# Overlapping slices, powers on GpSimd and half swaps by DMA in a fused scan-and-gate kernel

## The chip, the cores and the metric

The kernel runs on one core of one Trainium2 chip. The core has five engines that matter here. TensorE (PE in the profile) multiplies 128-row tiles and leaves sums in PSUM. VectorE (DVE) and ScalarE (ACT) do elementwise work. GpSimd (POOL) does small elementwise work. SyncE (SP) issues transfers. Each has its own stream of instructions, and they meet only through semaphores. The metric is the time of one execution on the device in microseconds; of the kernel before there are three runs, and one more execution was recorded by the profiler.

## What is computed

```python
xn = layernorm(x)                                  # x: 2048 x 448, bf16
# the scan (448 complex states, diagonal)
dt      = exp(log_dt);  Lam_bar = exp(dt * Lam)
B_bar   = ((Lam_bar - 1) / Lam)[:, None] * B
h[t]    = Lam_bar * h[t-1] + B_bar @ xn[t]
s       = 2 * real(C @ h) + xn * Dskip
# the gate (two dense layers of 448 -> 1792 -> 448)
g       = silu(gelu(layernorm(xn) @ w1 + b1) @ w2 + b2)
out     = x + s * g
```

The second layernorm of an already normed row differs from the first only in its factor, since `eps` enters twice. So the kernel takes the mean and variance of x once and forms two factors from them. The rows scaled by the first factor (`xn`) go into the scan, those scaled by the second (`xm` in the names, `xn2` in the buffers) into the gate.

## The kernel before

**Tiles.** The 2048 rows are worked on in four groups `g` of 512. A group is two blocks `b` of two tiles `r` with 128 rows each. The width 448 is three and a half tiles of 128. Where it is the contracted dimension, columns 0 to 383 fill three tiles, and the last 64 columns stand in the fourth tile twice, once in each half of the partitions. `halved` (L663) then runs the product in pairs of matmuls on 64 of the 128 partitions: a first pass over all four tiles for one half, a second over three for the other, so that the 64 doubled columns count once. It serves the w1 products (`mm1`, `mm1_half`) and the first three tiles of the B projection (`bu`).

**The doubled columns** come from more transfers and copies: `ldxe` loads columns 384 to 447 of x a second time, `dup` (L432) copies them on GpSimd for the first tiles, `ldw1` (L381) loads the last 64 rows of w1 in two transfers for each of four chunks, and the tails of B are loaded narrow, doubled on GpSimd, and transposed by a DMA of their own in `bt` (L638).

**Stages of a group.** The norms (`ln_stats`, `ln_scale`, `ln_apply`; `first_norm` for the first block of group 0); transposes of xn and xm (`xt`), by TensorE or by a transposing DMA; the B projection in four steps (`bu`, named `U{g}{i}`); the scan (`ssm`): two products of all states with cosine and sine tables `WT`, a sum, seven scans along the 512 rows (L710), a copy of the scanned states to bf16 (`s_b`, L715), two products back and a sum into `h_sb`; the w1 products in seven steps of two column tiles each (`mm1`, named `H{g}{j}`; for group 0 in halves, `H0{j}{b}`), each followed by gelu on ScalarE into `gT`; the w2 products (`mm2`, 14 matmuls of 448 columns for each tile of rows, L777) after a pair of small matmuls that put b2 in the bank (L772), then silu; and the outputs (`ym`): seven matmuls with `CQ` and four with the diagonal tiles `DG` of Dskip (L798, L801), times g, plus x, and a store.

**The fourth tile of states** holds only 64 complex states. Their real part fills one half of the partitions and their imaginary part the other. A complex product then needs the two halves in swapped places as well. Before, ScalarE makes the swapped copy by two half copies of 64 partitions: from PSUM after `bu(g, 3)` (L692, L693), and from `s_f` after the scan (L717, L718). `bu(g, 3)` is eight half-column matmuls (L689).

**Parameters.** `parameters` (L522) turns the vectors by tiny matmuls and works out the decay and the angle of each state, mostly on GpSimd: exp(dt) and the modulus `R1` by Exp on ScalarE (L539, L546), sines by a polynomial. `first_norm` forms 1/sqrt(variance) by Ln and Exp on ScalarE (L446, L447), `ln_scale` by a power on GpSimd (L477) or by an iteration on VectorE. `tables` (L596) makes `WT` on VectorE and by five Sin instructions on ScalarE. Ln/Exp, gelu and sine/silu belong to three table sets of ScalarE, and each change of set is an `ACT_TABLE_LOAD`.

**Order.** Each call only records a `Task` with what it reads and writes. `emit` then issues the tasks in the order of a list written out by hand, `ORDER`. An entry is the number of a task, or its name: `H{g}{j}`, `U{g}{i}`, `T0` (transposes of `first_norm`), `I0` and `I1` (matmuls on zeros, with no reader), `ST` and `DH`. Each engine works through its own tasks in that order. `SECOND` lists the tasks that take their second alternative, for instance VectorE in place of ScalarE. `BANKS` gives each PSUM tile its bank. A task waits for the last of what it depends on, the earlier users of its bank among it. SP issues nearly all transfers, in the order of the list. So one that waits holds those behind it.

Of the kernel before, what the change touches and what calls it, by code (L numbers as in the profile page):

```python
# [200 lines left out]
18 ST I0 0 10 12 1 24 19 14 17 23 22 29 30 31 20 28 21 27 83 84 25 44 13 26 16 15 82 89 90 32 33 34 42 88 2 3 4 85 91 86 T0 94 92 T1 35 41  # L201
43 36 47 45 87 7 I1 40 38 39 93 H040 98 97 100 H050 114 H010 46 63 96 48 116 99 101 102 103 H000 115 37 108 117 H020 106 H030 79 95 109 110
104 107 111 H060 112 136 134 135 118 113 171 137 8 53 119 105 5 49 50 52 H051 H001 130 131 11 242 H011 120 H021 122 139 H031 124 121 51 H041
123 126 125 241 6 H061 155 170 127 138 158 159 62 143 141 142 140 144 128 129 161 55 56 57 58 218 160 162 132 246 243 240 247 245 133 146
145 148 223 221 224 244 147 54 329 248 333 327 149 153 150 258 225 259 151 157 156 226 219 220 227 U02 U00 193 152 U01 249 252 189 191 328
331 255 250 251 326 253 254 222 330 61 64 DH 68 173 194 154 192 H11 332 256 H16 71 334 190 292 415 414 257 413 172 165 338 H13 163 174 167
H14 293 296 419 412 297 417 197 198 260 298 418 302 H15 168 195 303 299 166 335 300 164 H12 196 65 H10 294 78 416 199 60 339 U12 206 290 265
301 295 U10 304 291 203 266 336 66 67 69 72 73 70 75 74 77 76 204 205 U11 207 202 261 340 80 175 344 177 262 169 200 337 178 201 176 208 209
214 181 309 263 307 310 311 211 179 264 308 305 213 420 180 183 312 H26 H22 388 210 182 185 306 H20 215 184 270 313 H25 376 216 186 217 421
269 422 389 345 380 H23 271 377 187 188 386 381 382 424 59 212 425 267 9 81 234 230 268 383 277 236 387 278 228 341 276 274 279 342 275 423  # L210
426 H32 346 237 272 231 H33 464 466 235 H31 229 H35 273 462 281 285 280 465 467 463 343 282 U22 286 U20 351 287 347 352 238 U21 470 349 288
232 348 H21 239 289 350 283 471 356 H30 H24 378 379 460 284 H34 384 461 385 395 468 355 357 360 353 316 322 314 354 320 396 363 361 362 398
364 365 323 358 317 430 427 428 429 359 321 431 432 315 366 U32 U31 437 469 367 371 397 399 372 368 U30 324 373 374 438 369 370 435 433 436
434 442 375 H36 474 390 472 473 479 325 233 393 439 441 440 443 318 447 450 406 475 476 394 400 408 451 448 446 449 444 453 407 445 452 454
319 455 456 402 480 391 477 392 457 458 459 482 403 401 404 405 484 483 481 478 409 486 485 410 490 411 487 488 491 492 494 495 489 493 496
498 499 500 501 497
""".split()]
SECOND = [int(k) if k.isdigit() else k for k in """
45 135 212 248 258 259 284 334 335 336 338 339 341 342 344 345 370 421 422 427 428 430 431
""".split()]  # L220
BANKS = [int(k) if k.isdigit() else k for k in """
0 3 1 0 2 0 6 2 6 4 0 4 0 2 6 0 2 4 6 4 0 6 4 0 4 2 3 4 5 2 6 3 7 0 6 4 2 6 2 0 4 6 2 0 2 3 4 5 7 5 4 6 4 6 0 4 2 0 6 0 6 4 0 6 7 0 1 2 7 3
4 0 6 4 2 4 6 0 4 2 2 2 4 5 0 1 2 3 2 0 1
""".split()]
B2_PE = tuple(range(16))


LN_EPS = 1e-5
# [8 lines left out]
def bass_recurrent_scan__ssm_conv_s5__mixer_channel_mlp__prompt_kernel(  # L237
# [14 lines left out]
    NB, NG, NF, NK = 8, 4, 14, 512  # L252
# [3 lines left out]
    with ExitStack() as es:  # L256
# [3 lines left out]
        ident = SB("ident", [128, 128])  # L260
        still = SB("still", [128, 128])
        mhalf = SB("mhalf", [128, 1, 1], F32)
        sgn = SB("sgn", [128, 4], F32)
        cw = SB("cw", [128, 26, 4], F32)

        ang = SB("ang", [128, 5, 2, 2, 4], F32)
# [64 lines left out]
        with nc.Block():  # L331
# [42 lines left out]
            def ldxe(b0, n, reads=()):  # L374
                ldx(b0, n, reads, True)
# [528 lines left out]
```

## Time and profile before

| | us |
|---|---|
| three runs: median (lowest to highest) | 151.18 (150.34 to 151.41) |
| the profiled execution: its span | 148.9 |
| median less span | 2.3 |
| 0 to 7.96 us: PE / ACT / DVE / POOL busy | 5.29 / 4.22 / 4.74 / 3.06 |
| 7.96 to 21.00 us | 12.99 / 10.27 / 10.13 / 5.10 |
| 21.00 to 42.80 us | 20.97 / 21.68 / 12.91 / 6.46 |
| 42.80 to 138.60 us | 95.77 / 82.12 / 94.32 / 30.48 |
| 138.60 to 148.90 us | 7.57 / 1.42 / 6.80 / 0.00 |

The profiled execution has no device time of its own beside its span; the span begins and ends with the first and last recorded work, and the device time of a run also holds what lies around it. The stretches are cut where the first w1 matmul starts (7.96), at the end of the first w1 stage (21.00), where VectorE starts the products of the scan (42.80) and where the last state is nearly done (138.60). The costliest groups of instructions in the page, beside those shown with the prediction, are these:

```profile
L668 PE MATMUL psum<-xn2T,w_sb 64*128 64x512 bf16 (+1 forms) x490 | 46.3, 342 | 1.1 <-DVE lnmv L429 1.1
...
L710 DVE TENSOR_TENSOR_SCAN s_f<-cw,cur,v_sb 128x512 f32<-128x512 f32 x21 | 25.3, 1265 | 0.5 <-POOL cur L728 0.4
L798 PE MATMUL psum<-CQ,h_sb 128*128 128x448 bf16 (+2 forms) x119 | 24.7, 342 | 0.0
L668 PE MATMUL psum<-xnT,BT 64*128 64x512 bf16 x168 | 19.8, 377 | 0.5 <-DMA BT<-in_A_B_im_dram 0.4
```

Left of the bar stand the line, the engine, the operation, the written tile and the read tiles, the sizes and the count. Then come the busy time of the group in us, the mean of one in ns, and the idle time of the engine ahead of the group with what ended most of it. The w1 products (46.3 us), the w2 products (43.4 us), the outputs (24.7 us) and the B projection (19.8 us) are TensorE's work; the scans on VectorE are 25.3 us of its 128.9.

### The profile page before, as it was taken

How to read it: one execution, taken by the hardware profiler on the slowest of the kernel's cores; microseconds unless marked ns; L12 is line 12 of the kernel's file. 1: busy time of each engine (PE TensorE's matmuls, PEld its weight loads, DVE VectorE, ACT ScalarE, POOL GpSimd, SP SyncE). 2: the span in 40 equal slices, each digit the busy share in tenths (PEclk: the TensorE clock that was granted, in tenths of full speed). 3: DMA queues.
4: the chain of work that ended last, by engine and by line, in shares of the span. 5: the costliest groups of instructions: out<-in, count | busy, mean ns of one | idle time of the engine just before them, and what ended most of it. 6: DMA issues, size and time to landing. Idle time of an engine off the chain costs nothing.

```text
span 148.9 us, 3017 instructions
## 1 busy us (share of the span) xinstructions
PE 142.6 (96%) x1156; PEld 77.3 (52%) x1156; DVE 128.9 (87%) x198; ACT 119.7 (80%) x181; POOL 45.1 (30%) x84
## 2 busy tenths in 40 slices
PE   7789989998999999999999999999999999999992
PEld 2378975544554445545455545545544445555562
DVE  2983999950479999999999999989999999999874
ACT  2738999999999999999999999989799855291300
POOL 3360547800004999996000000930003700000000
PEclk9959999999999999999999999999999999999999
DMA  4789999969988530000324301000702101000033
GB/s 108 206 251 233 343 255 142 149 117 178 189 144 124 105 72 0 0 0 4 70 45 95 70 4 61 0 7 0 141 0 67 62 0 62 0 0 4 8 118 123
DMA packets 32767, 13.25 MB, mean 89 GB/s; under 512 B 25960, under 2 KB 32368, under 8 KB 32752
## 3 DMA queue, kind: packets, MB, share of 16 engines
q1 hardware_dynamic: 32592, 12.98, 41.9%
q8 instruction: 9, 0.15, 0.4%
q10 hardware_dynamic: 160, 0.07, 0.2%
q14 instruction: 6, 0.05, 0.1%
HBM read 5.82 MB, written 1.84 MB: 51 GB/s over the span
## 4 chain that ended last, share of the span: by engine, by line
PE 78%; ACT 7%; POOL 4%; DVE 4%; DMA 2%; issue 2%; ACTq 1%; SPq 1%; DVEq 0%; POOLq 0%
PE psum L668 37%; PE psum L777 21%; PE psum L798 14%; ACT gT L761 5%; PE psum L689 3%; DMA BT<-in_A_B_im_dram 2%; PE psum L801 2%; ACTq L107 1%; POOL cw L564 1%; SPq L106 1%; ACT L341 1%; DVE t L804 1%; DVE lnst L425 1%; PE psum L772 1%; DVE tmp L808 1%
## 5 line engine op out<-in xcount | busy, mean ns | idle before, releaser
L668 PE MATMUL psum<-xn2T,w_sb 64*128 64x512 bf16 (+1 forms) x490 | 46.3, 342 | 1.1 <-DVE lnmv L429 1.1
L777 PE MATMUL psum<-w_sb,gT 128*128 128x448 bf16 x224 | 43.4, 353 | 0.4 <-DMA w_sb<-in_B_w_dram 0.4
L668 PEld LDWEIGHTS psum<-xn2T,w_sb 64*128 64x128 bf16 x490 | 28.0, 110 | 17.5 <-issue 1.3
L777 PEld LDWEIGHTS psum<-w_sb,gT 128*128 128x128 bf16 x224 | 21.6, 98 | 21.5 <-DMA w_sb<-in_B_w_dram 0.8
L749 ACT ACTIVATE gT<-psum,b1f 128x512 bf16<-128x512 f32 x42 | 25.5, 689 | 0.4 <-PE psum L668 0.3
L710 DVE TENSOR_TENSOR_SCAN s_f<-cw,cur,v_sb 128x512 f32<-128x512 f32 x21 | 25.3, 1265 | 0.5 <-POOL cur L728 0.4
L798 PE MATMUL psum<-CQ,h_sb 128*128 128x448 bf16 (+2 forms) x119 | 24.7, 342 | 0.0
L668 PE MATMUL psum<-xnT,BT 64*128 64x512 bf16 x168 | 19.8, 377 | 0.5 <-DMA BT<-in_A_B_im_dram 0.4
L725 POOL TENSOR_TENSOR cwk<-s_f,ang 128x8 f32<-128x8 f32 x3 | 4.2, 1408 | 39.7 <-ACT s_f L722 39.5
L715 ACT ACTIVATE s_b<-s_f 128x3072 bf16<-128x3072 f32 x4 | 11.0, 2760 | 4.7 <-DVE s_f L710 4.7
L798 PEld LDWEIGHTS psum<-CQ,h_sb 128*128 128x128 bf16 x119 | 10.4, 98 | 7.4 <-issue 0.5
L425 DVE BATCH_NORM_STATS2 lnst<-x_all 128x6 f32<-128x448 bf16 x14 | 8.1, 612 | 6.8 <-DMA x_all<-in_A_x_dram 6.8
L668 PEld LDWEIGHTS psum<-xnT,BT 64*128 64x128 bf16 x168 | 8.1, 94 | 10.8 <-issue 1.6
L781 ACT ACTIVATE g_sb<-psum 128x448 bf16<-128x448 f32 x16 | 8.0, 537 | 6.7 <-PE psum L777 6.7
L761 ACT ACTIVATE gT<-psum,b1f 128x256 bf16<-128x256 f32 x28 | 11.1, 471 | 2.8 <-PE psum L668 2.8
L685 ACT ACTIVATE u_sb<-psum 128x1024 bf16<-128x1024 f32 x12 | 11.8, 1025 | 0.2
L564 POOL TENSOR_TENSOR cw<-cw 128x4 f32<-128x4 f32 x11 | 4.8, 445 | 19.7 <-DVE lnmv L429 17.0
L804 DVE TENSOR_TENSOR t<-psum,g_sb 128x448 bf16<-128x448 f32 (+2 forms) x17 | 9.7, 589 | 1.3 <-PE psum L798 1.3
L499 ACT ACTIVATE xn_sb<-x_all,lnw 128x512 bf16<-128x512 bf16 x13 | 10.3, 809 | 0.1
L710 DVE TENSOR_TENSOR_SCAN s_f<-cw,v_sb 128x512 f32<-128x512 f32 x7 | 8.2, 1213 | 0.0
L498 DVE TENSOR_SCALAR xn_sb<-x_all,lnw 128x512 bf16<-128x512 bf16 x17 | 6.5, 404 | 1.5 <-issue 1.3
L732 DVE TENSOR_TENSOR pa<-s_b,WT 128x3072 bf16<-128x3072 bf16 x4 | 7.0, 1750 | 0.4 <-ACT s_b L715 0.4
(131 smaller groups left out, 184.7 us busy)
## 6 DMA issues: line engine op xcount, KB each, us to landing
out_dram<-tmp SPq DMA_DIRECT2D x7, 224.0 KB, 2.1
x_all<-in_A_x_dram SPq DMA_DIRECT2D x3, 448.0 KB, 5.3
w_sb<-in_B_w_dram SPq DMA_DIRECT2D x3, 448.0 KB, 8.2
w_sb<-in_B_w_dram SPq DMA_DIRECT2D x3, 384.0 KB, 4.8
w_sb<-in_B_w_dram SPq DMA_DIRECT2D x6, 64.0 KB, 4.0
x_all<-in_A_x_dram SPq DMA_DIRECT2D x2, 112.0 KB, 2.1
x_all<-in_A_x_dram SPq DMA_DIRECT2D x1, 224.0 KB, 3.0
w_sb<-in_B_w_dram SPq DMA_DIRECT2D x1, 224.0 KB, 5.8
```

What stands on the lines that cost most here:

```text
L425: dve([lambda e, b=b, r=r, q=q: e.bn_stats(lnst[:, q, :], x_all[:, xa(2 * g + b, r), 0:D])], [f"x{2 * g + b}"] + (["xmT0p1"] if (g, b) == ...
L499: ("act", lambda e: e.activation(dst, src, ACT.Identity, bias=nb, scale=rs), 0.81)]
L668: return lambda e: e.matmul(out(k), wt(k, d, halves[h]), rhs(k, d, halves[h]), start=first and d == 0, stop=not first and d == 2)
L685: act(lambda e: e.activation(u_sb[:, i, :, :], psum[:, bank.b:bank.b + 2, :], ACT.Copy), [bank.key], [f"u{i}"], 1.02)
L710: dve(lambda e, i=i, ri=ri, init=init: e.tensor_tensor_scan(s_f[:, i, ri, :], col(R1, i).to_broadcast([128, NK]), v_sb[:, i, ri, :], init, ...
L715: act(lambda e: e.activation(s_b[:, 0:3, :, :], s_f[:, 0:3, :, :], ACT.Copy), SF, ["sb"] + early, 2.76)
L749: act([lambda e, k=k: e.activation(gT[:, gb, 2 * j + k, :], psum[:, bank.b + k, :], ACT.Gelu_apprx_tanh, bias=b1f[:, 2 * j + k:2 * j + k + ...
L761: act([lambda e, k=k: e.activation(gT[:, 0, 2 * j + k, :].rearrange("p (r c) -> p r c", r=2)[:, :, cs], psum[:, bank.b + k, :].rearrange(" ...
L777: fns = [lambda e, fi=fi, bk=bk, q=q: e.matmul(psum[:, bk.b, 0:D], gT[:, gb, fi, q * 128:(q + 1) * 128], w2_sb[:, fi, :], start=(fi == 0 a ...
L781: act(lambda e, gs=gs, bk=bk: e.activation(g_sb[:, gs, :], psum[:, bk.b, 0:D], ACT.Silu), [bk.key] + (["silu"] if g == 0 else []), [f"g{gs ...
L798: fns = [lambda e, k=k: e.matmul(psum[:, bank.b, c0:c1], h_sb[:, hb, k, k0:k0 + 128], CQ[:, k, c0:c1], start=(k == 0), stop=(k == 6)) for ...
L804: dve(lambda e: e.tensor_tensor(t3[:, ob, r, c0:c1], psum[:, bank.b, c0:c1], g_sb[:, gs, c0:c1], ALU.mult), [bank.key, f"g{gs}"], [f"t3{ob ...
```

## The change

**Overlapping slices.** The contracted dimension is no longer cut into 3.5 tiles with the half doubled. It is read as columns 0 to 255 and 192 to 447, two overlapping windows of 256, which make four full tiles; columns 192 to 255 are the doubled ones. x is stored 448 wide, w1 and B are loaded in two such slices, and the narrow loads and the copies on GpSimd go. `halved` leaves out the doubled half at another place. The w1 chunks are cut 2, 4, 4, 4 column tiles wide, not 4, 4, 4, 2.

```diff
-            CH = ((0, 4), (4, 4), (8, 4), (12, 2))
+            def win(ap):
+                return bass.AP(tensor=ap.tensor, offset=ap.offset, ap=[ap.ap[0], [192, 2], [1, 256]])
+            CH = ((0, 2), (2, 4), (6, 4), (10, 4))
...
-                ld("sp", w1_sb[:, 0:3, a:a + w], dram_ap(B_w1, a, [[F, 128], [128 * F, 3], [1, w]]), [f"w1_{c}"], 384 * w * 2, dur=0.5)
-                for h in range(2):
-                    ld("sp", w1_sb[h * 64:h * 64 + 64, 3, a:a + w], dram_ap(B_w1, 384 * F + a, [[F, 64], [1, w]]), [f"w1r{h}_{c}"], 64 * w * 2, dur=0.5)
+                for k in range(2):
+                    ld("sp", w1_sb[:, 2 * k:2 * k + 2, a:a + w], dram_ap(B_w1, 192 * k * F + a, [[F, 128], [128 * F, 2], [1, w]]), [f"w1_{c}_{k}"], 256 * w * 2, dur=0.5)
...
-                other = [half(k, d, 1 - k) for d in range(3) for k in (1, 0)]
+                other = [half(k, ds[k], 1 - k) for ds in ((0, 0), (2, 1), (3, 3)) for k in (1, 0)]
```

The four transposing loads of B move up into the list of plain loads and need no copy first. The second tile of the first block of x goes by ScalarE's queue, and the second block follows ahead of w1. In `ym` the diagonal tiles cover columns 0, 128, 256 and 320 on, the third of them 64 wide.

**Norms of group 0.** `first_norm` treats four tiles, not two, each with a scale and a power on GpSimd, and the factors of xn are one more chain there. ScalarE's Ln and Exp go, and so does the VectorE chain of the second block.

```diff
-                    kb.add("act", [lambda e, var=var, r1=r1: e.activation(r1, var, ACT.Ln, scale=1.0 + LN_EPS, bias=eps[:, 1:2]),
-                                   lambda e, r1=r1: e.activation(r1, r1, ACT.Exp, scale=-0.5)], [f"mv0_{q}", "eps", "warm"], [f"r1{r}"],
-                           dur=0.53, chain=True, table="exp")
+                        kb.add("pool", [lambda e, var=var, w0=w0: e.tensor_scalar(w0, var, 1.0 + LN_EPS, LN_EPS * LN_EPS, op0=ALU.mult, op1=ALU.add),
+                                        lambda e, w0=w0, r1=r1: e.tensor_tensor(r1, w0, mhalf[:, 0, :], ALU.pow)], [f"mv0_{q}", "mhalf"], [f"r1{q}"],
+                               dur=0.5, chain=True)
...
+                for k in range(1, 5):
+                    idle = kb.psum()
+                    kb.tag = f"I{k}"
+                    pe([lambda e, idle=idle: e.matmul(psum[:, idle.b, 0:128], still[:, :], still[:, :], start=True, stop=True) for _ in range(8)], ["still"], [idle.key], 0.5)
```

`I1` to `I4` are four groups of eight matmuls on zeros where one stood. Group 1's `ln_scale` moves from VectorE to GpSimd. The xn transposes of group 0 go from transposing DMAs to TensorE. Of the seven w1 steps of group 0, the first two are still done in halves and the other five whole.

**No exponential table.** exp(dt) and `R1` become powers of e on GpSimd; the first table loaded is gelu's.

```diff
-            act(lambda e: e.preload_act_table_set("natural_log_exp_and_others"), [], ["warm"], 1.3, "exp")
+            preload("gelu_apprx_tanh_and_others", [], "warm", "gelu")
...
-                act(lambda e: e.activation(col(DT), col(LDT), ACT.Exp), ["cp", "warm"], ["cdt"], 0.2, "exp")
+                pool(lambda e: e.tensor_tensor(col(DT), euler[:], col(LDT), ALU.pow), ["cp", "euler"], ["cdt"], 0.25)
```

**Tables.** Two sines over the whole array replace five; the third table is the negative of the first, by VectorE or ScalarE. To allow this, the angle of the fourth tile's lower states changes its sign ahead of the sine.

```diff
+                act(lambda e: e.activation(WT[:, :, 0, :], ra, ACT.Sin, scale=TWO_PI), RA + ["silu"], ["W0"], 1.98, "silu")
+                act(lambda e: e.activation(WT[:, :, 1, :], rb, ACT.Sin, scale=-TWO_PI, bias=sgn[:, 3:4]), ["rb", "sgn3", "silu"], ["W1"] + RA + ["rb", "iota"], 1.98, "silu")
+                kb.either(("dve", lambda e: e.tensor_scalar(WT[:, :, 2, :], WT[:, :, 0, :], -1.0, None, op0=ALU.mult), 0.68),
+                          ("act", lambda e: e.activation(WT[:, :, 2, :], WT[:, :, 0, :], ACT.Copy, scale=-1.0), 1.98), ["W0"], ["W2"])
```

**The last states.** The last 64 columns of the real and imaginary B are copied side by side into `BT3`, with the doubled half set to zero, and `bu(g, 3)` becomes four matmuls on the full array. The swapped halves, of the projection and of the scanned states, come from two DMAs each on SP.

```diff
-                    pe([colhalf(d, k) for d in range(4) for k in range(2)], rd, [bank.key], 1.0)
-                    act([lambda e: e.activation(u_sb[:, 3, 1, :], psum[:, bank.b, :], ACT.Copy),
-                         lambda e: e.activation(u_sb[halves[0], 3, 0, :], psum[halves[1], bank.b, :], ACT.Copy),
-                         lambda e: e.activation(u_sb[halves[1], 3, 0, :], psum[halves[0], bank.b, :], ACT.Copy)],
-                        [bank.key], ["u3"], 1.8)
+                    pe([lambda e, d=d: e.matmul(psum[:, bank.b, :], BT3[:, d, :, :].rearrange("p k c -> p (k c)"), xr[:, d, :, :], start=(d == 0), stop=(d == 3)) for d in range(4)],
+                       rd, [bank.key], 0.87)
+                    kb.either(("act", lambda e: e.activation(u_sb[:, 3, 1, :], psum[:, bank.b, :], ACT.Copy), 0.6),
+                              ("dve", lambda e: e.tensor_copy(u_sb[:, 3, 1, :], psum[:, bank.b, :]), 0.6), [bank.key], ["u3s"])
+                    swap(u_sb, 1, 0, "u3s", "u3", [])
+            def swap(buf, a, b, rd, wr, early):
+                for k in range(2):
+                    kb.dma("sp", buf[halves[k], 3, b, :], buf[halves[1 - k], 3, a, :], reads=[rd], writes=[f"{wr}{k}"] + early, nbytes=65536)
```

**More choices and a new order.** The copies of `u_sb`, of the transposes, of the parameters and of the fourth tile's states may now go to ScalarE or to VectorE. `ORDER`, `SECOND` and `BANKS` are new throughout. The fixed alternative in which VectorE adds b2 goes (no group used it). The last tile of rows does its columns 256 to 447 ahead of 0 to 255.

More of the change, by code (lines that the diff above doesn't have):

```diff
@@ L678, in bu @@
                 gx = g % 2
-                rd = [f"xnT{gx}_{b}" for b in range(2)] + BTK[i]
+                rd = [f"xnT{gx}_{b}" for b in range(2)] + (BTK if i < PK else ["BT3"])
                 bank = kb.psum(2 if i < PK else 1)
@@ L768, in mm2, with half @@
                 bank = [kb.psum() for _ in range(2)]
-                onpe = 4 * g + 2 * b in B2_PE
-                if onpe:
-                    def half(r):
-                        return lambda e: e.matmul(psum[:, bank[r].b, 0:D], mean64[halves[r], :], b2bc[halves[r], :], start=True, stop=False)
-                    pe([half(r) for r in range(2)], ["mean64", "b2bc"], [bank[0].key, bank[1].key], 0.25)
+                def half(r):
+                    return lambda e: e.matmul(psum[:, bank[r].b, 0:D], mean64[halves[r], :], b2bc[halves[r], :], start=True, stop=False)
+                pe([half(r) for r in range(2)], ["mean64", "b2bc"], [bank[0].key, bank[1].key], 0.25)
                 for r in range(2):
@@ L841, in bass_recurrent_scan__ssm_conv_s5__mixer_channel_mlp__prompt_kernel @@
             for b in range(2):
[L842 removed]
+                xt(0, b, 0, "pe")
             tables()
```

270 lines of the change are left out of this document (116 added, 154 removed).

## The prediction

> **What bounds the kernel now.** I read the page's first two parts, then TensorE's waits, the chain that ended last in order of time, and stretches and rows of the timeline.
>
> ```profile
> span 148.9 us, 3017 instructions
> PE 142.6 (96%) x1156; PEld 77.3 (52%) x1156; DVE 128.9 (87%) x198; ACT 119.7 (80%) x181; POOL 45.1 (30%) x84
> ```
> ```profile
> PE psum L668 <- DVE lnmv L429: 1.1, 1, 1.1
> PE psum L668 <- DMA BT<-in_A_B_im_dram: 0.4, 1, 0.4
> PE psum L777 <- DMA w_sb<-in_B_w_dram: 0.4, 1, 0.4
> ```
> ```profile
> 7.96 4.35 PE psum L668 x50
> ...
> 30.37 3.62 DMA BT<-in_A_B_im_dram
> ...
> 44.88 1.10 PE psum L689 x8
> 45.98 6.17 PE psum L668 x56
> ...
> 144.67 0.64 DVE t L804
> ...
> 146.76 0.26 DVE tmp L808
> ```
> ```profile
> 4.13:7.54 3.41, 2.21 (x29) 1.39 (x27) 3.07 (x9) 2.55 (x11) 1.09 (x4) 1.00 0.76 198
> 7.54:10.95 3.41, 2.99 (x30) 2.58 (x32) 3.00 (x15) 1.02 (x3) 2.30 (x12) 0.50 0.88 245
> ...
> 21.00:54.69 33.69, 32.86 (x261) 16.24 (x256) 24.80 (x61) 33.48 (x47) 14.19 (x29) 1.00 0.90 138
> 42.84:138.60 95.76, 95.73 (x714) 47.53 (x711) 94.28 (x98) 82.08 (x116) 30.48 (x27) 1.00 0.21 42
> ```
> TensorE works without a gap of note from 7.96 us to its last matmul near 146. Only two gaps after 7.96 have names (0.4 and 0.4 us, both on DMA). So time can be won in four places: before 7.96, in the stretch at clock 0.50 (TensorE had 2.21 of 3.41 us busy before it), in the two gaps, and in TensorE's own work. VectorE is close behind: from the first product of the scan (42.84) to the last of the state, it is busy 94.28 of 95.76 us, and it ends 1.3 us before TensorE needs the result:
> ```profile
> 42.84 1.73 DVE L702 TENSOR_TENSOR pa<-u_sb,WT 128x3072 bf16<-128x3072 bf16 x1
> ...
> 138.17 0.42 DVE L736 TENSOR_TENSOR h_sb<-pa 128x512 bf16<-128x512 bf16 x1
> ...
> 139.91 0.35 PE L798 MATMUL psum<-CQ,h_sb 128*128 128x448 bf16 x1
> ```
>
> **The start.** Before, the first w1 matmul waits for the w1 load (the wait is put down to VectorE, which had long delivered its tiles). After, the wanted w1 piece is small and early, and four tile norms come first.
> ```profile
> 2.92 0.63 DVE L444 BATCH_NORM_STATS2 lnst<-x_all 128x6 f32<-128x448 bf16 x1 [1.93 <-DMA x_all<-in_A_x_dram]
> ...
> 4.31 0.18 DVE L445 BATCH_NORM_AGGREGATE lnmv<-lnst 128x2 f32<-128x6 f32 x1
> 4.76 0.83 DVE L449 TENSOR_SCALAR xn_sb<-x_all,lnmv,lnw 128x512 bf16<-128x512 bf16 x2 [0.26 <-ACT lnw L447]
> ...
> 5.66 0.84 DVE L455 COPY xn2T<-psum 128x512 bf16<-128x512 bf16 x2
> ```
> ```profile
> 7.97 0.23 POOL L462 TENSOR_SCALAR lnw<-lnw 128x2 f32<-128x2 f32 x1
> ...
> 55.90 2.04 POOL L477 TENSOR_TENSOR lnw<-lnw,mhalf 128x8 f32<-128x8 f32 x1
> ```
> Two tiles' statistics take VectorE 2.92 to 4.49, so four end near 6.1. The new order puts all four ahead of the first scaling. Four scalings at 0.41 end at 7.8, and the copy of tile 2's transpose at 8.25. The first w1 matmul, which also stands behind the fourth transpose, starts at about 8.35: 0.4 later than before. Each tile's factor is now a scale and a power on GpSimd. A small GpSimd instruction is 0.23; the one power in the trace is 2.04, for 8 columns, in a busy stretch. So a pair costs 0.5 to 2.3; with one column and little beside it I take 0.6. Then the factors come at 4.4, 5.2, 5.9 and 6.7, each ahead of its scaling. Ln, Exp and their table leave ScalarE, which waits there anyway: nothing. x tile 1 moves to ScalarE's DMA queue, ahead of six small loads that only delays the parameters, with about 1 us to spare.
>
> The Trainium skill (GPSIMD Engine Reference, section 8 Key points) speaks against such a move: elementwise work is about twice as fast on VectorE, and GpSimd shares its SBUF interfaces with it. The 0.23 against 2.04 us above agrees that company can be dear; taking the skill's factor of two alone for the pair would leave the sum as it is, since 0.6 has 0.7 us of room.
>
> **Clock.** 50 half-width matmuls took 4.35 us at the low clock. At full clock:
> ```profile
> 14.02 0.62 PE L514 MATMUL psum<-ident,xn_sb 128*128 128x128 bf16 x8
> ...
> 14.57 6.29 PE L668 MATMUL psum<-xn2T,w_sb 64*128 64x256 bf16 x112
> ...
> 21.97 8.31 PE L777 MATMUL psum<-w_sb,gT 128*128 128x448 bf16 x43 [0.41 <-DMA w_sb<-in_B_w_dram]
> ```
> 112 take 6.29, so 50 take 2.8: 1.55 us lost. The change adds three idle-filling groups of eight matmuls (0.6 us each) and TensorE then works about 3.1 of the 3.4 us before its first w1 step. I take full clock.
>
> The Trainium skill (TensorE: Matmul & The Clock Gate, Part 1) says that the clock falls after an idle window of some 3.4 us and that the window runs free of the kernel. Here the trace does not agree with the first: 2.21 of 3.41 us were busy and the clock fell to 0.50 all the same. By the second, the same gaps could be punished in one run and not in another: that is the rival "low clock again".
>
> **The first w1 stage.** Four half-width steps (4 x 7 pairs x 0.112) and five full ones (5 x 7 x 0.220, the 56 in 6.17 us above) are 10.85; the sixteen transposes of xn that TensorE takes over from DMA (about 0.5 for each eight) and two bias pairs (0.2 each) are 1.35. TensorE is through at 8.35 + 12.2 = 20.55. ScalarE must follow:
> ```profile
> L749 ACT ACTIVATE gT<-psum,b1f 128x512 bf16<-128x512 f32 x42 | 25.5, 689 | 0.4 <-PE psum L668 0.3
> ...
> L761 ACT ACTIVATE gT<-psum,b1f 128x256 bf16<-128x256 f32 x28 | 11.1, 471 | 2.8 <-PE psum L668 2.8
> ...
> L499 ACT ACTIVATE xn_sb<-x_all,lnw 128x512 bf16<-128x512 bf16 x13 | 10.3, 809 | 0.1
> ```
> From the end of the fourth step's matmuls (13.05) it has four full pairs (2 x 0.69, by overlap down to 1.2), two scalings (0.81) and one half pair (0.8) up to the gelu that the w2 product needs: 20.3 to 21. The table load before the first gelu falls in ScalarE's wait for step 4. So the w2 product starts at 20.55 instead of 21.97: **-1.4**. Its data must be there:
> ```profile
> GB/s 108 206 251 233 343 255 142 149 117 178 189 144 124 105 72 0 0 0 4 70 45 95 70 4 61 0 7 0 141 0 67 62 0 62 0 0 4 8 118 123
> ```
> Slices are 3.72 us: 4.24 MB by 18.6. The new queue has 4.47 MB up to the end of w2 (x 0.92, w1 1.83, b2 0.11, w2 1.61): 19.5 at these rates, 1 us ahead. The narrow column copies of x, the B tails and their two GpSimd copies go; they are off the path, so nothing. The four B transposes (0.92 MB) now wait for nothing on SP and land near 27, against 34 before; TensorE comes to them at 31.2. So the 0.42 gap goes: **-0.4**. What is late next is ScalarE.
>
> **The fourth projection.** Eight half-column matmuls are 1.10. Four full ones are, by
> ```profile
> L777 PE MATMUL psum<-w_sb,gT 128*128 128x448 bf16 x224 | 43.4, 353 | 0.4 <-DMA w_sb<-in_B_w_dram 0.4
> ```
> 0.194 x 512/448 x 4 = 0.89. Four groups: **-0.85**. The copy to BT3 and its memset lie on ScalarE and VectorE ahead of need (31 us against 35).
>
> **Half swaps.** ScalarE loses two copies per swap; SP gains 16 DMAs.
> ```profile
> L717 ACT ACTIVATE s_b<-s_f 64x512 bf16<-64x512 f32 x4 | 2.5, 628 | 0.0
> ...
> L749 ACT ACT_TABLE_LOAD x3 | 3.8, 1283 | 0.1
> ```
> ```profile
> out_dram<-tmp SPq DMA_DIRECT2D x7, 224.0 KB, 2.1
> ...
> h_sb<-h_sb SPq DMA_TRANSPOSE x1, 3.8
> ```
> A swap of this kind isn't in the trace: 2.1 to 3.8 us with its issue, once for each of 8 swaps. I take 2.1, the plain copy. Its reader on VectorE stands behind three wide products (3 x 1.75 = 5.2 us), so it is hidden; were it not, up to 3.8 us a group. Behind the waiting swaps on SP stand x transposes and output stores, all with microseconds to spare. ScalarE saves 8 x 1.2 = 9.8 us and three table loads (11 become 8), 3.85 us, and takes on seven more scalings, 5.7 us. That is worth only the waits it prevents.
>
> **The middle.** These rows give ScalarE's load there:
> ```profile
> L685 ACT ACTIVATE u_sb<-psum 128x1024 bf16<-128x1024 f32 x12 | 11.8, 1025 | 0.2
> ...
> L781 ACT ACTIVATE g_sb<-psum 128x448 bf16<-128x448 f32 x16 | 8.0, 537 | 6.7 <-PE psum L777 6.7
> ...
> L632 ACT ACTIVATE tmp<-h_sb,cw 128x448 f32<-128x448 bf16 x6 | 4.0, 667 | 0.1
> ...
> L615 ACT ACTIVATE WT<-s_f,sgn 128x2048 bf16<-128x2048 f32 x1 | 2.0, 1998 | 0.0
> ```
> From 21.0 to the gelu that frees the second w2 product's bias banks it has two sines 4.0, an absolute value 1.9, eight gelu pairs 9.6, eight scalings 6.5, five u copies 5.1, four silus 2.1, three C scalings 2.0, two table loads 2.6 and small copies 1.4: 35.2, so 56.2. TensorE, from 20.55, is there at 57 if it never waits. That is nearly a tie, and single banks come late: walking the order I find 0.3 us at the last w1 step of group 1 and 0.5 us at the first of group 2. Before, TensorE was idle for 0.83 of the 33.69 us of this stretch, all of it in the two named gaps. I take **+0.8** for all new waits; ends 0 and 2.5. GpSimd's norm of group 1 (five small instructions, 1.4 to 7 us, after VectorE's 2.2) is wanted at 22.5 and comes between 18 and 23.5; that is inside these ends. VectorE starts its products near 39.3 instead of 42.84 and keeps the same 95 us, so it stays ahead of TensorE. W2 as a negative of W0 adds 0.7 to VectorE ahead of its start. The tail (144.67 to the end) is the same work in the other column order: 0.
>
> **Sum.** -1.4 - 0.4 - 0.85 + 0.8 = -1.85: span 147.05. The median of the runs is 151.18, 2.3 above the span: **149.3 us**, range of this case 148.2 to 149.9.
>
> **Rivals.** *ScalarE paces the middle.* The tie above says for it, that the old order had ScalarE just as full (33.48 of 33.69) and still let TensorE run says against. At 2.5 instead of 0.8 the time is 151.0; the case covers 149.9 to 151.5. *Low clock again.* Then the 50 matmuls cost 1.55 more: 150.8; the fuller window speaks against. *Slow powers* (slower). One power per tile, four in a row on GpSimd, gate the fourth transpose and so the first w1 step. At 2.04 + 0.23 each the fourth factor comes at 13.0, the stage starts at 14, 5.6 later: 154.9. It turns into a loss where a pair exceeds 1.35 us. For it: the 2.04 row; against: that row had 8 columns and neighbours of 0.75 to 1.67 us in the same stretch, where quiet ones are 0.23. *No waits at all*: 148.2 or less.
>
> **How the numbers follow.** Forecast 0.53, ScalarE 0.21, low clock 0.07, slow powers 0.14, no waits 0.05. One per cent is 1.5 us, about what a measurement of this kernel can tell from no change: faster below 149.7, slower above 152.7. The part of the forecast under 149.7 (0.47) and "no waits" make faster 0.52; the rest of it (0.06), ScalarE and low clock make same 0.34; slow powers make slower 0.14. The range 148.0 to 151.5 leaves out slow powers and half of "no waits".
>
> **What would show it.** Right: first w1 matmul at 8.0 to 8.8 with PEclk 9 in slices 2 and 3; w2 product from 20 to 21; no wait on BT; the fourth projection at 0.9; swap landings near 2 us that nobody waits for. Wrong: small GpSimd rows above 1.3 us before 7 us, PE waits on gelu or u copies of more than 1.5 us between 37 and 60, or a clock of 0.50 after 8 us.

## The result, and the profile after

| | us |
|---|---|
| before, beside it on the same chip: median (lowest to highest) | 150.76 (150.09 to 151.41) |
| after: median (lowest to highest) | 156.7 (156.49 to 157.95) |
| ratio after / before, 95% interval | 1.041 (1.035 to 1.047) |
| span of the profiled execution, before / after | 148.9 / 155.0 |

The change makes the kernel 4% slower; 149.3 was predicted. Single executions far above all others (301.6 us once in `together` below, 518.93 once in the kernel before beside `copy`) are left out of the ratios. First the two lines of the page, then four stretches (start and end in us, length, busy time of PE, PEld, DVE, ACT and POOL with their instructions, granted clock, DMA share, GB/s). They answer to the stretches shown before.

```profile
span 155.0 us, 2903 instructions
PE 147.9 (95%) x1114; PEld 73.4 (47%) x1114; DVE 127.2 (82%) x176; ACT 106.1 (68%) x150; POOL 41.7 (27%) x94
```
```profile
4.13:7.54 3.41, 3.41 (x28) 1.58 (x27) 3.11 (x10) 0.61 (x2) 2.43 (x7) 1.00 0.96 290
7.54:10.95 3.41, 3.20 (x50) 2.41 (x50) 2.26 (x6) 2.38 (x5) 2.95 (x11) 1.00 1.06 343
21.00:54.69 33.69, 32.74 (x260) 15.59 (x256) 22.22 (x49) 29.59 (x41) 12.11 (x34) 1.00 0.62 106
42.60:145.10 102.50, 100.71 (x724) 47.98 (x720) 95.08 (x95) 74.61 (x103) 17.42 (x18) 1.00 0.22 45
```

The clock is whole from the start. The last stretch runs from VectorE's first wide product to its last state, as the 95.76 us one did before. It has grown by 6.7 us, and VectorE does 95.08 us of work in it against 94.28. ScalarE does 7.5 us less and GpSimd 13. So no engine has much more to do, and TensorE is called busy for 100.71 of 102.50 us. This is where the whole loss lies:

| us from the start of the span | before | after | predicted |
|---|---|---|---|
| first w1 matmul | 7.96 | 9.41 | 8.35 |
| first w2 product | 21.97 | 23.88 | 20.55 |
| first wide product of VectorE | 42.84 | 42.60 | 39.3 |
| last state of group 0 ends | 69.05 | 71.14 | |
| of group 1 | 92.84 | 100.30 | |
| of group 2 | 118.17 | 123.36 | |
| of group 3 | 138.59 | 145.09 | |

Three answers of the waits view say what is new. The first fence is TensorE's weight loads after (waiting engine and tile, releaser; total us, times, longest). The second and third fences are VectorE's waits from its first product to its last state, after and before.

```profile
PEld psum L652 <- PE psum L652: 13.7, 27, 0.6
```
```profile
DVE pa L719 <- DMA s_b<-s_b: 2.9, 1, 2.9
DVE CQ L625 <- ACT tmp L622: 1.3, 2, 0.9
DVE pa L716 <- ACT s_b L700: 1.3, 1, 1.3
DVE tmp L796 <- DMA out_dram<-tmp: 0.6, 1, 0.6
```
```profile
DVE s_f L710 <- POOL cur L728: 0.4, 1, 0.4
DVE pa L732 <- ACT s_b L715: 0.4, 1, 0.4
DVE CQ L635 <- ACT tmp L632: 0.2, 1, 0.2
```

The first row has no counterpart before. A step of `halved` records two tasks: the named one, eight matmuls in which each half of the array adds to its own bank, and a numbered one, six matmuls with the halves crossed. The second writes the banks of the first, so it waits for TensorE's own semaphore, which the last matmul of the first pass raises. In the old order another task always stood between. In the new `ORDER` the two stand side by side at 27 places. These are starts of single matmuls in the trace at one of them:

```
42.568  42.571      last two of the first pass
43.012  43.016      first two of the second pass: 0.441 us later
43.255  43.261      the next two: 0.243 us later
43.471  43.476      0.216 us
```

Two matmuls start every 0.216 us when nothing waits (42.352 and 42.568 in this first pass), so a place costs 0.441 - 0.216 = 0.225 us, 0.23 below; 27 of them are 6.1. By its modelled end the last matmul of the first pass is over at 42.947, and the second pass starts 0.065 us behind that. The weight loads' row gives 0.5 each, because a load otherwise starts ahead of its matmuls: 0.21 us ahead of those at 42.568, 0.004 ahead of those at 43.012. The row of matmuls shows none of it: their ends are modelled, and PE stays "busy".

That 27 times 0.23 comes so near to the whole loss is in part chance. Nine of the places stand ahead of the first w2 product, and 18 in the stretch that has grown by 6.7 us: they are 4.1 us of it.

So there were two theories. P: TensorE's 27 waits for itself set the pace, and all else follows. V: VectorE's waits for late copies (5 us above the old ones) are the price, wait by wait.

### The profile page after: what moved, and what is told of

It is laid out like the page before. It is cut to its first block, busy times and chain, and to the rows that moved or that the text cites. A ratio compares the mean times of both kernels' runs of the same rounds, so it can differ in the third digit from the quotient of the medians.

```text
span 155.0 us, 2903 instructions
## 1 busy us (share of the span) xinstructions
PE 147.9 (95%) x1114; PEld 73.4 (47%) x1114; DVE 127.2 (82%) x176; ACT 106.1 (68%) x150; POOL 41.7 (27%) x94
## 4 chain that ended last, share of the span: by engine, by line
PE 56%; DVE 26%; DMA 5%; ACT 5%; issue 4%; SPq 1%; DVEq 0%; ACTq 0%
PE psum L652 30%; PE psum L759 14%; DVE s_f L696 10%; PE psum L776 3%; DMA out_dram<-tmp 3%; DVE t L783 3%; DMA s_b<-s_b 3%; DVE v_sb L690 2%; DVE pa L688 2%; PE psum L804 2%; DVE pb L689 2%; ACT gT L733 2%; PE psum L455 2%; DVE pa L719 1%; SPq L107 1%
## 5 line engine op out<-in xcount | busy, mean ns | idle before, releaser
L652 PE MATMUL psum<-xn2T,w_sb 64*128 64x512 bf16 (+1 forms) x420 | 48.3, 364 | 1.3
L733 ACT ACTIVATE gT<-psum,b1f 128x512 bf16<-128x512 f32 x52 | 32.4, 692 | 4.9 <-PE psum L652 4.8
L652 PEld LDWEIGHTS psum<-xn2T,w_sb 64*128 64x128 bf16 x420 | 21.4, 109 | 26.2 <-PE psum L652 10.3
L652 PE MATMUL psum<-xnT,BT 64*128 64x512 bf16 x168 | 20.7, 377 | 1.0 <-ACT gT L733 0.6
L709 POOL TENSOR_TENSOR cwk<-s_f,ang 128x8 f32<-128x8 f32 x3 | 1.5, 499 | 52.1 <-ACT s_f L706 52.1
L494 ACT ACTIVATE xn_sb<-x_all,lnw 128x512 bf16<-128x512 bf16 x20 | 15.5, 809 | 0.0
L422 DVE BATCH_NORM_STATS2 lnst<-x_all 128x6 f32<-128x448 bf16 x12 | 7.1, 612 | 2.5 <-DMA x_all<-in_A_x_dram 2.5
L690 DVE TENSOR_TENSOR v_sb<-pa,pb 128x3072 bf16<-128x3072 bf16 x4 | 7.0, 1757 | 0.1
L718 DVE TENSOR_TENSOR h_sb<-pa,pb 128x3072 bf16<-128x3072 bf16 x4 | 7.0, 1757 | 0.1
L688 DVE TENSOR_TENSOR pa<-u_sb,WT 128x3072 bf16<-128x3072 bf16 x4 | 7.0, 1752 | 0.0
```

Source lines behind the costliest of these rows:

```text
L494: ("act", lambda e: e.activation(dst, src, ACT.Identity, bias=nb, scale=rs), 0.81)]
L652: return lambda e: e.matmul(out(k), wt(k, d, halves[h]), rhs(k, d, halves[h]), start=first and d == 0, stop=not first and d == 3)
L688: dve(lambda e: e.tensor_tensor(pa[:], wide(u_sb, 0), WT[:, 0:3, 1:3, :], ALU.mult), U + WK, ["pa"], 1.76)
L690: dve(lambda e: e.tensor_tensor(v_sb[:, 0:3, :, :], pa[:], pb[:], ALU.add), ["pa", "pb"], ["v"], 1.76)
L733: act([lambda e, k=k: e.activation(gT[:, gb, 2 * j + k, :], psum[:, bank.b + k, :], ACT.Gelu_apprx_tanh, bias=b1f[:, 2 * j + k:2 * j + k + ...
```

## The experiments

The diffs of orders show TensorE's or ScalarE's tasks alone, and a short piece of them.

**Take the pairs apart** (17 moves in TensorE's order).

```diff
-H20 362 H21 364 H25 372 291 292
+H20 H21 362 364 H25 291 372 292
```

> The changed kernel with 17 tasks of its order moved by a place or two, so that no task of TensorE stands directly behind the one whose result it adds to; nothing else differs. In the changed kernel this is so 27 times, and the trace shows a start-to-start gap 0.227 us above the cadence at each. Drain theory: 27 x 0.227 = 6.1 us of TensorE's time come back, the gaps are gone from the trace, and the time falls from 156.7 to 149.8 to 151.5. Swap theory (VectorE's 2.94 us wait for a swapped half at 97.6 us is a price of its own, and the drains hide behind VectorE): at most 3 us come back and the wait stays, 153.5 or more. Late-start theory (powers and x landing later set the loss): within 1% of 156.7.

157.83 us, ratio 1.045 (1.039 to 1.052). Of the 27 waits one is left (of 1.3 us), and the time is no better. TensorE's own waits in this kernel:

```profile
PE psum L652 <- ACT gT L733: 3.2, 4, 1.5
PE psum L652 <- ACT u_sb L669: 0.5, 1, 0.5
PE psum L754 <- ACT u_sb L669: 0.3, 1, 0.3
```

A step that starts earlier needs its PSUM bank earlier, and the bank is freed by a gelu or a copy that ScalarE reaches in its own order. P in its simple form (take the pairs away, get the time back) falls.

**Half swaps by ScalarE again**, in the changed order.

```diff
-                    kb.dma("sp", buf[halves[k], 3, b, :], buf[halves[1 - k], 3, a, :], reads=[rd], writes=[f"{wr}{k}"] + early, nbytes=65536)
+                    act(lambda e, k=k: e.activation(buf[halves[k], 3, b, :], buf[halves[1 - k], 3, a, :], ACT.Copy), [rd], [f"{wr}{k}"] + early, 0.62)
```

> The changed kernel with the half swaps done by ScalarE's half copies again in place of the two DMAs each; the order and the 27 adjacent passes stay. Swap theory: the 2.94 us wait for a swapped half goes, 153 to 154.5. Drain theory: ScalarE takes on about 1.2 us for each of 8 swaps while TensorE still loses 6.1 us; the time stays between 155 and 158, and a wait of VectorE at that place stays, now on ScalarE.

163.09 us, ratio 1.083 (1.074 to 1.091), more than either theory allowed. VectorE now waits 7.04 us at one place:

```profile
76.16 0.69 DVE L719 TENSOR_TENSOR pa<-s_b,WT 128x1024 bf16<-128x1024 bf16 x1 [7.04 <-ACT s_b L680]
```

The swaps by DMA are not the loss. In this order they are worth 6.4 us.

**Pairs put into the kernel before** (23 moves, 27 places, all in the work of groups 0 and 1 that comes first).

```diff
-H11 H16 292 H13 H14 296 298 302 H15 195 300
+H11 292 H16 302 H13 296 H14 298 H15 300 195
```

> The kernel before with 23 tasks moved, so that the second pass stands directly behind the first at 27 places, all of them in groups 0 and 1, ahead of about 65 us; nothing else of the change is in it. Drain theory: 27 x 0.227 = 6.1 us are lost in the stretch in which TensorE sets the pace, 155 to 157.5, and the gaps show at each place. If adjacent passes cost nothing, or other engines hide them, it stays within 1% of 150.8.

157.03 us, ratio 1.035 (1.025 to 1.045). The weight loads' row of this kernel:

```profile
PEld psum L668 <- PE psum L668: 12.6, 27, 0.6
```

Nothing of the change is in this kernel but the pairs, and it loses 6.1 us beside a before of 150.92 on its chip (3.7 to 6.8 by the interval). Part of that may be the clock: in this profiled execution (157.06 us, mean clock 0.978) it was 0.50 for 6.83 us from 7.27 on, where the profile before has 0.50 for 3.41 us. Another run with 0.978 took 157.01; the one run at the whole clock took 154.85, 3.9 us more than 150.92. (Two runs of the kernel before that met as low a mean clock, 0.977, took 151.56 and 151.85.) And part of the way went through others: VectorE waits 3.9 us for a u copy and 2.7 us for a vector that GpSimd works out (`sx`).

**Only one side reordered, and all.** `peorder` reorders TensorE's tasks, `others` those of all engines but TensorE. `full` reorders all and changes engine choices and banks too, `beforeopt` does the same to the kernel before. A piece of TensorE's order in `peorder`, of ScalarE's in `others`, and of TensorE's in `full` and in `beforeopt`:

```diff
-H20 362 H21 364 H25 372 291 292 289 287 294
+H20 362 H21 H25 287 289 291 364 294 245 292
```

> The changed kernel; only TensorE's tasks stand in another order among themselves and the rest (banks, the alternatives and the order on every other engine as in the changed kernel). Adjacent passes fall from 27 to 8, and the second passes are put off only where their bank and ScalarE can bear it, which the first reordering (157.8 us) did not look at: there TensorE's named gaps on ScalarE grew from 0.6 to about 4 us. Drain theory: 19 x 0.227 = 4.3 us come back and reach the end, 151 to 153. ScalarE theory (the order of ScalarE and VectorE sets the time whatever TensorE does): within 1% of 156.7, as with the first reordering, with the gaps on ScalarE in place of the drains.

```diff
-285 244 275 240 363 185 327 186
+275 153 285 244 185 240 186 363
```

> The changed kernel; TensorE's order with its 27 adjacent passes is kept, and the tasks of VectorE, ScalarE, GpSimd and SP are reordered instead, so that the copies which VectorE waits for (C scalings, scanned states, swapped halves) come earlier. ScalarE theory: VectorE's 6.7 us of named waits after 42.6 us mostly go, and the time falls to 150.5 to 153. Drain theory: TensorE stays 6 us short, and at most 1 to 2 us come back, 154.5 to 156.5.

```diff
-H12 H15 H13 278 H14 276 282 U11 241 H10 280
+H13 H12 278 276 H15 H14 282 280 U11 H10 241
```

> The changed kernel with every part of the change, but another order on all engines, other banks for 31 tiles and another choice of engine for 28 tasks. If the order is the cause of the loss and not the parts, it is faster than the changed kernel by 6 to 9 us: 147.5 to 150.5, at or below the kernel before. If a part of the change (powers, swaps, full-array last states, the cut of w1) costs the time, it stays above 153.

```diff
-H11 H16 292 H13 H14 296 298 302 H15 195
+H11 189 292 H13 H16 296 H14 302 298 H15 195
```

> The kernel before with none of the change's parts, its order, banks and choices of engine worked over in the same way as those of the kernel in the run above. It tells what the parts are worth at equal care for the order. If the parts are worth the 1.9 us of the prediction, it stays at 149.5 to 151 and above the reordered changed kernel; if they are worth nothing, both come to the same time within 1 us, 147.5 to 149.5.

| | median | ratio (95%) | what is late |
|---|---|---|---|
| peorder | 154.91 (153.98 to 156.57) | 1.027 (1.020 to 1.035) | VectorE 4.12 us at 96.19 for the swapped half of group 1 |
| others | 158.92 | 1.056 (1.051 to 1.061) | VectorE 2.9 us for `s_b`, 1.9 us for a u copy; 1.7 us for a store in the tail |
| full | 159.58 | 1.061 (1.054 to 1.067) | TensorE 5.3 us for a parameter load moved behind large ones |
| beforeopt | 153.09 | 1.019 (1.013 to 1.026) | TensorE 3.0 us for such a load |

`peorder` has 9 of the waits left and wins some 2 us of the 4.3 that its first theory gave. `others` is slower than either theory allowed. `full` and `beforeopt` settle nothing: their small loads were moved behind w1, and that spoiled the start. After them, the DMA issues were left where they are.

**The swap of group 1.** It is VectorE's longest wait. In the changed kernel the scan was done at 89.0 us, and these rows of ScalarE's timeline show its copy (L701) behind a u copy and four gelus that wait for TensorE:

```profile
88.70 1.02 ACT L669 ACTIVATE u_sb<-psum 128x1024 bf16<-128x1024 f32 x1
90.16 1.02 ACT L669 ACTIVATE u_sb<-psum 128x1024 bf16<-128x1024 f32 x1 [0.43 <-PE psum L652]
91.93 2.42 ACT L733 ACTIVATE gT<-psum,b1f 128x512 bf16<-128x512 f32 x4 [0.74 <-PE psum L652]
94.22 0.65 ACT L701 ACTIVATE s_b<-s_f 128x512 bf16<-128x512 f32 x1
```

The copy is moved up, in the changed kernel (`copy`) and in peorder (`pecopy`). ScalarE's tasks in `copy`:

```diff
-330 334 461 375 262 332 453 265
+330 262 265 334 461 375 332 453
```

> The changed kernel with one chain moved up: in group 1 ScalarE's copy of the fourth scanned state, the two half swaps behind it and the hand-over of the scan's ends go ahead of one u copy and two pairs of gelus; TensorE's and VectorE's order are as they were. In the changed kernel that scan ended at 89.0 us, its copy ran only at 94.22, its swaps landed at 97.48, and VectorE stood 2.94 us at 97.60. Theory V (VectorE's idle time is the price, wait by wait): the wait goes, 156.7 minus 2.9 = about 153.8, and every later state ends 2.9 us earlier. Theory P (TensorE with its 27 waits for its own first passes paces group 2 as well, and ScalarE behind it): the last state of group 1 ends 2 to 3 us earlier, but VectorE finds a new wait in group 2 for a copy that stands behind an activation that waits for TensorE; the time stays at 156 to 157.

> The kernel with TensorE's tasks reordered (peorder: 8 adjacent second passes instead of 27, 154.9 us) with the same chain moved up. There VectorE waited 4.12 us at 96.19 for the swapped half. If its waits are the price once TensorE is ahead (V and P both): 154.9 minus 4.1 = 150.8. If TensorE or ScalarE is late next here too: 153 to 155, with a new VectorE wait in group 2.

`copy`: 155.78 us, ratio 1.034 (1.028 to 1.041), 0.9 us won of 2.9. The wait went and the last state of group 1 ends 2.9 us earlier, at 97.38. But group 2's ends only 1.0 us earlier, because a new wait came (ScalarE and VectorE of `copy`):

```profile
111.06 0.54 ACT L762 ACTIVATE g_sb<-psum 128x448 bf16<-128x448 f32 x1 [4.58 <-PE psum L759]
111.50 2.75 ACT L700 ACTIVATE s_b<-s_f 128x3072 bf16<-128x3072 f32 x1
```
```profile
DVE pa L716 <- ACT s_b L700: 1.8, 1, 1.8
DVE tmp L796 <- DMA out_dram<-tmp: 0.6, 1, 0.6
```

VectorE waits for the copy of `s_b`, the copy stands behind a silu, and the silu waits 4.58 us for a w2 product: TensorE is late here too. `pecopy`: 154.95, ratio 1.028 (1.022 to 1.035), no better than peorder. V falls as a sum of single waits.

**Orders reworked, with and without TensorE's.** `feeds` leaves TensorE's order as it is and reworks ScalarE's, VectorE's and GpSimd's; `pefree` reworks TensorE's too. No instruction, engine choice, bank or DMA issue changes. A piece of TensorE's order in `pefree`:

```diff
-U11 241 H10 280 272 H11 274 H16 284 U12 243 U10 239 286 H20 362 H21 364 H25 372 291 292 289 287 294
+U11 280 241 H10 H11 272 H16 274 U12 284 243 U10 286 239 H20 362 H21 287 289 291 364 294 245 292 H25
```

> The changed kernel with TensorE's order untouched (all 27 adjacent second passes stay), no engine choice, PSUM bank or DMA issue changed, and the order of ScalarE, VectorE and GpSimd after the start reworked so that copies which VectorE waits for go ahead of gelus. V: the waits of 0.47, 0.88, 1.30 and 2.94 us and the 1.14 us of statistics ahead of the first product go, 156.7 minus 5 to 6 = 151 to 152. P: TensorE's order still sets the ends of the later groups, 154.5 to 156.5.

> As feeds, but TensorE's order is reworked as well (4 adjacent second passes left of 27); engine choices, PSUM banks, the start and the DMA issues are those of the changed kernel. If the parts of the change are sound and only the order of the four engines cost the time: under 151, at best the kernel before minus the 2 us that the first prediction's parts gave, 148 to 151. If the parts themselves cost (start 1.45 us later, swaps by DMA): 152 to 155.

`feeds`: 155.25 us, ratio 1.030 (1.024 to 1.037). VectorE's waits for the tmp copies and for `s_b` of group 0 are gone, and 1.4 us are won. `pefree`: 150.73 us, ratio 1.003 (1.002 to 1.005): all parts of the change at the time of the kernel before. So the 6 us that the change loses lie in the order, and 4.5 of them come only with TensorE's. Its row in `pefree`:

```profile
PEld psum L652 <- PE psum L652: 2.5, 5, 0.6
```

**Is it the pairs, or where else the steps stand?** `welded` reworks as `pefree` does, but keeps the 27 pairs whole. `rejoin` is `pefree` with 18 tasks moved, so that 29 pairs stand together; all other orders are untouched.

```diff
-U11 280 241 H10 H11 272 H16 274 U12 284 243 U10 286 239
+U11 241 280 H10 H11 274 272 H16 284 U12 243 U10 239 286
```

> As pefree, all four engines reordered in the same way after the start, with one rule more: the 27 second passes that stand directly behind their first passes stay there, and each pair moves as one. What tells it apart: if the adjacent pairs themselves cost (27 waits of TensorE for its own first pass, 6 us in the changed kernel, of which the 8 in the start stay in both), this ends 3.5 to 5 us above pefree's 150.7, at 154 to 156. If it was any other side of TensorE's order (which step stands when), it comes down with pefree to 150.5 to 152.

> pefree with 18 second passes moved two to five places up TensorE's order, directly behind (or first passes directly ahead of) their partners: 29 adjacent pairs instead of 4; every other engine's order, the banks, the DMAs and the instructions are pefree's. If each adjacent pair costs TensorE 0.227 us and TensorE sets the pace: up to 25 times 0.227 = 5.7 us more, 155 to 156.5 against pefree's 150.7. If the waits are hidden (VectorE paces from the first product on): 150.7 to 152.

`welded`: 158.83 us, ratio 1.053 (1.047 to 1.059). Its last state ends at 142.89, against 137.51 in `pefree`; another 2.4 us are lost behind it, where VectorE waits for stores. `rejoin`: 157.5 us, ratio 1.047 (1.042 to 1.052), 6.8 us over `pefree` (6.6 by the ratios, for they ran on different chips). Both are slower than their expectations for costly pairs. The weight loads, and three steps in a row in TensorE's timeline:

```profile
PEld psum L652 <- PE psum L652: 16.1, 30, 0.8
```
```profile
83.00 5.49 PE L652 MATMUL psum<-xn2T,w_sb 64*128 64x512 bf16 x42
88.33 3.88 PE L652 MATMUL psum<-xnT,BT 64*128 64x512 bf16 x30
```

Those 42 matmuls take 5.33 us from start to start, 1.78 for each step of 14. The 56 in 6.17 us of the kernel before are 1.54 each. The difference is 0.24 a step, and no gap is printed. 25 more waits at 0.23 are 5.8 us; the last 1.0 is not traced to one place (TensorE in `rejoin` has waits of 0.4 and 0.3 us for a gelu and a u copy that `pefree` lacks, and VectorE waits more for u and `s_b` copies and for a gelu). No run takes the wait away alone: the second pass adds to the banks of the first, and nothing else in the kernel orders the two. So its price is shown by moving passes only, and that also shifts what stands around them.

**What are the parts worth, and what does the start cost?**

`beforefree` is the kernel before, reworked as `pefree` was. `best` is `pefree` with engine choices and banks changed as well. In `start`, VectorE scales the first two tiles (85, 80) ahead of the statistics of the fourth (92, 93). A piece of TensorE's order in the first two, and of VectorE's in `start`:

```diff
-H11 H16 292 H13 H14 296 298 302 H15 195 300
+H11 191 292 H16 H13 H14 296 302 298 H15 195
```

> The kernel before, its four engines reordered in the same way as pefree's (start, DMA issues, engine choices and banks its own). It sets the measure for the parts of the change: pefree is 150.7. If the parts are worth the 1.5 us that the prediction summed, this stays at 151.5 to 152.5; if they cost as much at the start (1.45 us) as they bring, it comes to 149.5 to 151; if it falls under 149.5, the parts themselves cost.

```diff
-H13 H15 278 282 H12 H14 276 U11 280 241
+H13 204 278 H15 H12 282 276 U11 H14 H10 241
```

> pefree with 26 engine choices and the PSUM banks reworked as well (2 adjacent second passes left; start and DMA issues as in the changed kernel). Its VectorE still idles 2.45 us ahead of the first product and some 2 us in the tail in pefree: if those are what is left, 149 to 150; if ScalarE or TensorE is late next, as in full, 151 to 154.

```diff
-ST 82 83 77 78 87 88 92 93 80 85 90 95 86 96
+ST 82 83 77 78 87 88 85 80 92 93 90 86 95 96
```

> pefree with its start reordered too, DMA issues left where they are: the first two tiles are normalised and transposed ahead of the statistics of the third and fourth, so that the first w1 matmul stands about 0.6 us earlier than pefree's 9.43. If the later start is a price of the change by itself: 150.7 minus 0.6 = 150.1. If TensorE waits for weights or VectorE's chain instead: 150.7.

`beforefree`: 151.88, ratio 1.006 (1.000 to 1.012). The same rework does nothing for the old order. `best`: 152.76, ratio 1.013 (1.006 to 1.020). No version came in under the kernel before. `start`: the first w1 matmul stands at 8.67, not 9.43, and nothing is won: 150.92, ratio 1.003 (1.002 to 1.005). The first w2 product stays at 22.09 us in it (22.13 in `pefree`), so the later start is taken up before that point.

## Why the prediction was wrong, step by step

- **The failed step: "TensorE, from 20.55, is there at 57 if it never waits", with "+0.8 for all new waits".** The walk along the order looked at gelus, u copies and banks, and not at a second pass behind its own first pass. There are 27 such places at 0.23 us, 9 of them (2.0 us) ahead of the first w2 product. Where +0.8 stood for all new waits, these alone are 6.1 us of TensorE's time. `together` (+6.1 us, +3.9 in its one run at the whole clock) and `rejoin` (+6.8 us) show the price of this, put into the old kernel and into the reordered new one, and `pefree` shows the change with 5 such waits left. Taking the pairs apart without care for ScalarE's queue wins nothing (`apart`), and the queues reworked with the 27 waits in place win 1.4 us (`feeds`): the order failed as a whole, and the waits were the part of it that the walk did not look at. The signs of being wrong in the prediction did not find it either: GpSimd's small rows ahead of 7 us stayed at or under 0.58 us, TensorE's longest wait for a gelu was 0.6, and the clock was whole.
- **"ScalarE paces the middle", as a rival at 151.0,** had the right symptom, since all of VectorE's waits in the fence after but one (0.6 us for a store) have ScalarE ahead of them. But ScalarE was late by order, not by load: 74.61 us busy of 102.50. `apart`, `copy` and `pecopy` show that one queue put right uncovers the next.
- **The start: 8.35 forecast, 9.41 came.** The power was 0.55 to 0.58 us, near the 0.6 taken for a pair, but the scale ahead of it and two hand-overs make 0.92 from tile to tile:

```profile
5.77 0.19 POOL L440 TENSOR_SCALAR lnw<-lnmv 128x1 f32<-128x1 f32 x1
6.04 0.56 POOL L441 TENSOR_TENSOR lnw<-lnw,mhalf 128x1 f32<-128x1 f32 x1
6.69 0.19 POOL L440 TENSOR_SCALAR lnw<-lnmv 128x1 f32<-128x1 f32 x1
```

  The first two x tiles also landed 0.6 and 0.2 us later, at 3.46 and 3.63. "Slow powers" did not decide it: the pair stayed under its 1.35 us, and `start` takes 0.76 us of the delay away and gains nothing. The 2.04 us row that the prediction put down to company as well is mostly its 8 columns: after, powers of 1, 4 and 8 columns took 0.55 to 0.58, 1.02 to 1.05 and 1.66 to 1.83 us.
- **The first w1 stage, -1.4 us: +1.9 came.** Of the 3.3 us between, 1.06 are the start and 2.0 the nine waits. The length of the stage by itself was forecast well: 12.2 us, and in `pefree`, with two of these waits left in it, it took 12.70 (9.43 to 22.13). But an earlier start is not simply won: in `start` the stage took 13.42 without such a wait, and why is not traced. The clock came as forecast, 1.00 in both stretches. Yet the 1.55 us that it was to win back were no loss before. There the first w2 product, at 21.97, stood behind a load that landed at 21.93. And of the runs of the kernel before beside the experiments, 29 with a mean clock of 0.998 to 1.000 have a median of 150.5 us, and 16 with 0.987 to 0.989 (what one stretch of 3.41 us at 0.50 makes of 149 us) have 150.3. So the same kernel meets such a stretch in some runs and not in others; where it lay in each is not known.
- **The BT gap, -0.4: right.** TensorE's waits after have no row on BT. Only its weight loads show 0.4 us for the memset of `BT3`, which with the copy ahead of it ended at 34.22 and not near 31.
- **The fourth projection, -0.85 for four groups: right, 0.75 came.** From its first matmul to the next task's it takes 0.97, 0.86, 0.87 and 0.96 us; before it took 1.10 each time.
- **Half swaps: size right, cover wrong.** Of 16 transfers, 14 landed 1.9 to 2.2 us after their issue; 2.1 was taken. The three wide products that should hide them did so where the copy that feeds them came in time. In group 1 it stood 5.2 us behind the scan, and VectorE waited 2.94. Its price by itself was 0.9 us (`copy`).
- **VectorE "starts its products near 39.3" and "stays ahead of TensorE":** it started at 42.60, since its u copy waited 2.99 us for TensorE, and two statistics of a later group (1.14 us) stood ahead of the product. In `pefree` it starts at 39.98.
- **Table loads: 8 forecast, 9 came** (rows of 3, 2, 2, 1 and 1, 1.28 us each). The preload of gelu's set stands late in the order, so the first gelu loads it.

What stays open: whether the parts of the change are worth the 2 us that were summed. `pefree` and `beforefree` lie 1.2 us apart (0.5 by their ratios, for they ran on different chips), but neither order is known to be the best for its kernel. In `pefree` the last state ends at 137.51, 1.1 us earlier than before, but from there to the end of the span it takes 11.9 us against 10.3.

## What to carry to other kernels

When a list of tasks is reordered, read it per engine for neighbours of which the second needs the first: a wait for the engine's own semaphore costs each time (0.23 us on TensorE here), and a busy row can hide it. Compare the same step start to start, or look at the weight loads' waits. Where three engines with in-order queues run near their limits, moving one late task uncovers the next; test an order as a whole, and test a suspected cost from both sides, by taking it out and by putting it in.

## What the runs showed of the hardware

- A TensorE task that waits for TensorE's own last matmul starts 0.441 us after it (from start to start, 512 columns), where 0.216 us is the pace: 0.23 us for each wait. PE counts as busy meanwhile (95% after, 96% before), and the weight loads' row shows 0.5.
- A transfer of 64 KB within SBUF, half of the partitions to the other half, landed 1.9 to 2.2 us after its issue in 14 of 16 cases after the change. The first two took 3.4 and 3.1, and one in `peorder` 3.85; no row says why.
- A power on GpSimd takes longer with more columns: 0.55 to 0.58 us for one, 1.02 to 1.05 for four, 1.66 to 1.83 for eight after the change (2.04 for eight before).
- A stretch of 3.41 us at a clock of 0.50 need not cost this kernel time: its runs before the change have a median of 150.3 us with a mean clock of 0.987 to 0.989, and of 150.5 with 0.998 to 1.000.
